# Attention slots, idle products and early copies in a fused attention and double-MLP kernel

## The chip, the cores and the metric

The kernel runs on one core of a Trainium2 chip. A core has a matrix engine (TensorE, PE in the profile; PEld is its weight load), a vector engine (VectorE, DVE), an activation engine (ScalarE, ACT), GpSimd (POOL) and a sync engine (SP). Each runs its own queue of instructions in order and waits on semaphores for the others. Transfers are issued from the SP, ACT and POOL queues and carried by 16 DMA engines. The metric is device time in microseconds (us); lower is better. A profile is one execution recorded by the hardware.

## The reference

The inputs are float64 arrays; the MLP weights reach the kernel in that form and it takes them apart itself. The work, cut to what matters:

```python
# q, k, v: 4 batches, 8 heads, 576 positions, 64 wide
scores = q @ k.T / 8, kept where 0 <= row - column < 64, else -1e9
x = softmax(scores) @ v                        # to 2304 tokens x 512
x = (silu(x @ w_gate) * (x @ w_val)) @ w_out   # first MLP, 512 -> 1536 -> 512
out = (sigmoid(x @ w_gate2) * (x @ w_val2)) @ w_out2   # second MLP
```

## The kernel before

The 2304 tokens are 18 attention blocks of 128. The first MLP works on five tiles of 4, 3, 4, 4 and 3 blocks (`BLOCKS`, line 69): 512, 384, 512, 512 and 384 tokens, called tile 0 to tile 4 here. Every operand of a product is split into a high and a low part, and a product is three products of parts (high by high, low by high, high by low), each over four chunks: 12 matrix instructions for one gate, value or output step.

The first four blocks are computed ahead of tile 0, in the order that the string `START` writes out (two letters for a step, a number for the block; `wm` is a number of products on a tile of zeros that nobody reads, lines 899 to 901). From then on time is counted in *slots*. A tile has 36 of them, three for each of twelve feature chunks: gate product (slot number divisible by 3), value product, output product (of the chunk before). Slots run through tile 0 (0 to 35), tile 1 (36 to 71), tile 2 (72 to 107) and so on. Extra work is hung on a slot by `at(...)`: `before` is issued ahead of the slot's product, `during` right behind it, `after` behind the activation that follows. Within a list, entries with `first=True` come first. Since each engine runs its queue in order, a slot number fixes what stands ahead of what, not when it runs.

While one tile runs, the blocks of the next are prepared in its slots (`plan_attention`, line 500). With a block's base slot `base`: scores in `base+2` (`scores`, L246), masks on DVE (L265), exponentials on ACT (L283), division by the sums (`normalize`, L304 on ACT for blocks 4 to 7, L308 on DVE for others), transposes of the two weight halves on PE (`transpose_p`, L316) with a copy out on ACT (`evacuate_p`, L322), the product with the values (`pv`, L332), and the split of its result into x: the high half on ACT (`x_hi`, L342), then the low half on DVE (`x_lo`, L345), which needs the high one. Only after `x_lo` is the bank of `pv` free. Transposes, `pv` and scores share two PSUM banks named `att` in turn, so the fourth piece of a sequence such as transpose, transpose, pv, scores, scores waits until the pieces before it have been read.

For blocks 8 to 17, q and k are first copied in DRAM into a layout of 32 by 32 squares (`to_squares`, line 131; 16 copies for each of batches 1, 2 and 3, each of two DMAs of 128-byte runs) and turned by DVE (`turn`, L233). These copies, the raw weights (`load_raw`, L373, four buffers), the reloads of the first MLP's output words (`reload`, L421) and the stores of prepared words all go through SP's queue. The raw words of the second MLP's output matrix are fetched one by one in tile 1 (loop at line 657: load, conversion by ACT L391, L394 and DVE L404 to L406, store).

The second MLP follows tile 4 and is not touched.

Of the kernel before, what the change touches and what calls it, by code (L numbers as in the profile page):

```python
# [28 lines left out]
tk0 tq0 tq1 ek0 eq0 se0 so0 me0 mo0 tk1 xe0 eq1 tk2 ek1 ne0 so1 xo0 tq2 se1 ek2 mo1 ca0 no0 eq2  # L29
so2 xo1 pe0 po0 me1 we0 mo2 cb0 xo2 xe1 se2 me2 no1 wo0 wm2 ca1 no2 ne1 tq3 vp0 po1 tk3 pe1 ek3  # L30
ch0 ca2 cb1 eq3 wo1 vp1 so3 xe2 se3 mo3 me3 we1 ne2 xe3 pv0 hi0 po2 cl0 ch1 pv1 vp2 pe2 lo0 wm2
ne3 xo3 cb2 vp3 hi1 we2 lo1 no3 pe3 wm1 wo2 ca3 cb3 we3 ca4 pv2 hi2 po3 wo3 lo2 cb4 pv3 ch3 ca5
hi3 lo3 cb5 ch2 ch4 ch5 cl1 cl2 cl3 cl4 cl5
"""
SPLIT_EARLY = START.count("ca")
# [3 lines left out]
def attention_moe_moe(  # L39
# [301 lines left out]
    def x_hi(i, xt, col):  # L341
        nc.scalar.activation(out=xt[:, 0, :, col:col + 128], in_=st[i, "x"], func=ACTF.Copy)  # L342

    def x_lo(i, xt, col):
        nc.vector.tensor_tensor(  # L345
            out=xt[:, 1, :, col:col + 128],
            in0=st.pop((i, "x")),
            in1=xt[:, 0, :, col:col + 128].bitcast(FP32),
            op=ALU.subtract,
        )  # L350
# [88 lines left out]
    def x_tile():  # L439
        return x_p.tile([128, 2, CC, 512], FP32R, tag="x", name="x")  # L440
# [44 lines left out]
    before, during, after = {}, {}, {}  # L485
    xts = {}

    def x_of(t):
        if t not in xts:
            xts[t] = x_tile()  # L490
        return xts[t]

    def at(where, g, fn, *a, first=False):
        where.setdefault(g, []).append((not first, fn, a))
# [3 lines left out]
            fn(*a)  # L498

    def plan_attention(i, base, t, col):  # L500
        pv_at = 10 if t == 1 or (t > 2 and col == 0) else 9
        if base >= 2:
            at(during, base - (5 if i < TURN else 6), load_qk, i)
        at(during, base + 1 if i < TURN else base - 2, load_v, i)
        at(during, base + 5 if i <= TURN else base + 2, load_before, i)
        for nm in "qk":
            if i < TURN:
                at(before, base + 1, transpose_in, i, nm)
                at(before, base + 1, evacuate, i, nm)
            else:  # L510
                at(during, base - 1, turn, i, nm, first=nm == "k")
        at(before, base + 2, scores, i)
        at(after, base + 2, masked, i, 0, first=True)
        at(after, base + 3, masked, i, 1, first=True)
        at(after, base + 3, exps, i, 0, first=True)
        at(after, base + 3, exps, i, 1, first=True)
        at(after, base + (4 if i < TURN else 5), normalize, i, 0, first=i >= TURN)
        at(after, base + 5, normalize, i, 1, first=True)
        for par in range(2):
            at(before, base + 7 + par, transpose_p, i, par)  # L520
            at(before, base + 7 + par, evacuate_p, i, par)
        at(before, base + pv_at, pv, i)
        at(before, base + pv_at, lambda: x_hi(i, x_of(t), col))
        at(before, base + pv_at + 1, lambda: x_lo(i, x_of(t), col))


    for b in range(B):
        s = max(0, 128 * TURN - W - b * S)
        if s >= S:
            continue  # L530
        parts = [(nm, b, s, hp, par) for hp in range(HP) for par in range(2) for nm in "kq"]
        first = {1: 12, 2: 24, 3: 46}[b]
        for j, part in enumerate(parts):
            at(during, first + j, to_squares, *part)
    blk = BLOCKS[0]
    for t in range(NTL - 1):
        nb = BLOCKS[t + 1]
        for b in range(nb):
            plan_attention(blk + b, SPT * t + {4: 9 * b - 3, 3: 12 * b - (3 if t else 0), 2: 18 * b + 3}[nb], t + 1, b * 128)
        blk += nb  # L540
# [115 lines left out]

    for fc, g in enumerate((39, 41, 43, 46, 48, 50, 52, 57, 59, 61, 66, 68)):
        key = (1, "o", fc)
        at(during, g - 5, load_raw, key)
        at(during, g - 1, round_a, key)  # L660
        at(during, g, round_b, key)
        at(during, g + 1, store, key)
# [229 lines left out]
    with tc.manual_schedule():  # L892
# [4 lines left out]
        t = ps_m.tile([128, 512], FP32, tag="a3", name="warm")  # L897
# [8 lines left out]
        for step in LOADS.split():  # L906
            nm, j = step[0], int(step[1:])
# [43 lines left out]
        g = 0  # L951
# [87 lines left out]
```

## Time and profile before

| | us |
|---|---|
| median of 3 runs | 967.22 (966.86 to 968.52) |
| profiled execution, its own time | 967.57 |
| its span | 965.8 |
| PE busy | 944.8 (98%) |
| DVE busy | 616.1 (64%) |
| ACT busy | 464.2 (48%) |

The span is what the profiler sees between the first and the last instruction; the profiled execution took 1.8 us more than that. A busy PE is counted with modelled ends, so a product that waits for its predecessor still counts as busy. The chain of waits is followed back from the last instruction; a wait of PE is time that nothing else can give back, as long as no other engine sets the pace there.

### The profile page before, as it was taken

The page shows a single profiled execution, that of the slowest core. Times are in us where ns is not written, and L with a number is a line of the kernel's source. Part 1 is how long each engine was busy: PE and PEld are TensorE (multiplying, and loading weights), DVE is VectorE, ACT ScalarE, POOL GpSimd, SP SyncE. Part 2 cuts the span into 40 slices and gives each one's busy share as a digit, 9 for nine tenths or more (in the row PEclk, how much of TensorE's full clock was granted, in tenths as well). Part 3 has the DMA queues.
Part 4 walks back from the last instruction along what each step waited for, and adds up shares of the span by engine and source line. Part 5 has one row for each costly group of instructions (what it writes and reads, how often), then busy time and mean ns, then how long its engine had stood idle before and what let it go on. Part 6 is the DMA issues. An engine that isn't in the chain of part 4 may idle for free.

```text
span 965.8 us, 15744 instructions
## 1 busy us (share of the span) xinstructions
PE 944.8 (98%) x5693; PEld 843.4 (87%) x5693; DVE 616.1 (64%) x1401; ACT 464.2 (48%) x1042; POOL 21.1 (2%) x39
## 2 busy tenths in 40 slices
PE   8799999999999999999999999999999999999998
PEld 6678887899878887888899999998999988999986
DVE  6889984565756556555565566687366685566842
ACT  6798995755644556445444322145211343222332
POOL 2102010000000000000000000000000000000000
PEclk7899999999999999999999999999999999999999
DMA  9778897999786665865599557725787536866411
GB/s 223 208 230 251 265 242 213 307 231 280 246 256 187 206 207 170 288 217 159 196 351 362 200 203 275 259 58 162 259 287 232 189 92 205 300 223 243 142 33 65
DMA packets 191773, 210.62 MB, mean 218 GB/s; under 512 B 93136, under 2 KB 135632, under 8 KB 191696
## 3 DMA queue, kind: packets, MB, share of 16 engines
q1 hardware_dynamic: 185360, 199.27, 65.9%
q10 hardware_dynamic: 5376, 7.21, 2.1%
q0 software_dynamic: 960, 3.15, 1.1%
q8 instruction: 45, 0.74, 0.3%
q14 instruction: 32, 0.26, 0.1%
HBM read 168.69 MB, written 46.40 MB: 223 GB/s over the span
## 4 chain that ended last, share of the span: by engine, by line
PE 87%; ACT 8%; DVE 2%; DMA 2%; issue 1%; ACTq 0%; DVEq 0%
PE a L781 14%; PE g L448 13%; PE a L459 13%; PE v L448 12%; PE att L781 7%; PE a L846 7%; PE att L846 3%; PE v L781 3%; PE g L781 3%; PE g L846 3%; PE v L846 3%; ACT z L283 2%; PE att L332 2%; PE att L246 1%; DMA raw<-in_moe_w_out_dram 1%; ACT L283 1%
## 5 line engine op out<-in xcount | busy, mean ns | idle before, releaser
L448 PE MATMUL g<-x,wg 128*128 128x512 f32 (+1 forms) x720 | 161.0, 372 | 0.9 <-ACT x L342 0.8
L459 PE MATMUL a<-h,wo 128*128 128x512 f32 (+1 forms) x720 | 161.3, 372 | 0.0
L448 PE MATMUL v<-x,wv 128*128 128x512 f32 (+1 forms) x720 | 160.2, 371 | 0.0
L448 PEld LDWEIGHTS g<-x,wg 128*128 128x128 f32 x720 | 131.6, 189 | 19.8 <-ACT s L961 1.0
L459 PEld LDWEIGHTS a<-h,wo 128*128 128x128 f32 x720 | 129.5, 188 | 18.6 <-issue 1.9
L448 PEld LDWEIGHTS v<-x,wv 128*128 128x128 f32 x720 | 130.0, 188 | 16.3
L781 PE MATMUL a<-xs,wop 128*128 128x384 f32 x756 | 136.2, 334 | 0.0
L781 PEld LDWEIGHTS a<-xs,wop 128*128 128x128 f32 x756 | 131.5, 188 | 0.1
L968 DVE TENSOR_TENSOR s<-s,v 128x512 f32<-128x512 f32 (+1 forms) x60 | 38.0, 634 | 119.0 <-PE v L448 90.8
L773 ACT ACTIVATE s<-s 128x384 f32<-128x384 f32 x72 | 37.9, 526 | 81.9 <-DVE s L767 81.7
L781 PE MATMUL att<-xs,wop 128*128 128x384 f32 x384 | 71.7, 334 | 0.0
L846 PE MATMUL a<-wo,hs 128*128 128x512 f32 x288 | 71.2, 389 | 0.0
L961 ACT ACTIVATE s<-g 128x512 f32<-128x512 f32 (+1 forms) x60 | 33.3, 554 | 78.8 <-PE g L448 78.3
L970 ACT ACTIVATE h<-s 128x512 fp32r<-128x512 f32 (+1 forms) x60 | 35.1, 586 | 71.0 <-DVE s L968 70.8
L781 PEld LDWEIGHTS att<-xs,wop 128*128 128x128 f32 x384 | 67.1, 188 | 0.1
L846 PEld LDWEIGHTS a<-wo,hs 128*128 128x128 f32 x288 | 54.0, 188 | 11.1
L404 DVE TENSOR_SCALAR raw<-raw 128x512 uint16<-128x512 uint16 x72 | 54.6, 759 | 4.3 <-ACT raw L391 4.0
L283 ACT ACTIVATE z<-z,nm 128x128 f32<-128x128 f32 x144 | 55.8, 390 | 2.3 <-DVE nm L265 2.1
L391 ACT ACTIVATE raw<-raw 128x512 int32<-128x512 uint32 x72 | 48.4, 672 | 7.3 <-DMA raw<-in_moe_w_out_dram 5.5
L406 DVE CUSTOM_DVE_ANT_0 t<-raw,t 128x1024 uint16<-128x1024 uint16 x72 | 49.9, 694 | 2.5
L767 DVE TENSOR_TENSOR s<-s,a 128x384 f32<-128x384 f32 x65 | 35.1, 553 | 22.9 <-PE a L781 22.6
L430 ACT ACTIVATE wo<-tw 128x512 fp32r<-128x512 f32 x36 | 22.6, 627 | 54.1 <-PE a L846 26.0
(130 smaller groups left out, 1290.6 us busy)
## 6 DMA issues: line engine op xcount, KB each, us to landing
wop<-wd SPq DMA_DIRECT2D x126, 512.0 KB, 6.0
wo<-k0o SPq DMA_DIRECT2D x48, 512.0 KB, 4.9
wd<-stage SPq DMA_DIRECT2D x36, 512.0 KB, 5.1
raw<-in_moe_w_gate_dram SPq DMA_DIRECT2D x24, 512.0 KB, 5.5
raw<-in_moe_w_val_dram SPq DMA_DIRECT2D x24, 512.0 KB, 5.6
raw<-in_moe_w_out_dram SPq DMA_DIRECT2D x24, 512.0 KB, 5.1
tw<-k1o SPq DMA_DIRECT2D x36, 256.0 KB, 3.5
k0o<-wo ACTq DMA_DIRECT2D x12, 512.0 KB, 4.6
```

The source lines that it names most:

```text
L283: nc.scalar.activation(out=z[:, hp, :], in_=z[:, hp, :], func=ACTF.Exp, scale=-1.0, bias=nm[:, hp:hp + 1], accum_out=su[:, hp:hp + 1],)
L391: nc.scalar.activation(out=lower, in_=lower.bitcast(UINT32), func=ACTF.Copy, scale=2.0 ** -29)
L404: nc.vector.tensor_scalar(second, fourth, 0x8000, None, ALU.bitwise_and)
L406: nc.vector.tensor_tensor(out=t, in0=t, in1=lower, op=ALU.add)
L448: nc.tensor.matmul(out=ps[:, 0:n], lhsT=w[:, a, c, :], rhs=xt[:, b, c, 0:n], start=(j == 0), stop=(j == len(mm) - 1),)
L459: nc.tensor.matmul(out=acc[e][:, 0:n], lhsT=w[:, a, e * 128:(e + 1) * 128], rhs=h[:, b, 0:n], start=(fc == 0 and j == 0), stop=(fc == FC - ...
L767: nc.vector.tensor_tensor(out=to[out], in0=to[a], in1=ps, op=ALU.add)
L773: nc.scalar.activation(out=to[which], in_=to[which], func=ACTF.Sigmoid)
L781: nc.tensor.matmul(out=ps, lhsT=w[:, val, a, c, :], rhs=xops[op, b][:, c], start=(n == 0), stop=(n == len(mm) - 1),)
L846: nc.tensor.matmul(out=acc[e], lhsT=h[e // 3][:, a, e % 3 * 128:(e % 3 + 1) * 128], rhs=w[:, b], start=(fc == 0 and n == 0), stop=(fc == F ...
L968: nc.vector.tensor_tensor(out=s, in0=s, in1=vps[:, 0:n], op=ALU.mult)
L970: nc.scalar.activation(out=h[:, 0, 0:n], in_=s, func=ACTF.Copy)
```

## The change

Six things are edited. (1) `START`: six idle products ahead of block 3's `pv`, three behind it. (2) Transposes of the weights: in tile 1's slots (blocks 7 to 10) both halves in `base+8` instead of `base+7` and `base+8`, and `pv` in `base+10` instead of `base+9`; for the first block of tiles 3 and 4 (blocks 11 and 15) one slot later each. (3) `pv` of block 6, the last block prepared in tile 0, in slot 33 instead of 34. (4) `x_lo` of blocks 6 to 17 first in `during` of the slot of `pv`, instead of `before` the next slot. (5) The copies in squares: batch 1 in slots 10 to 24 (was 12 to 27), batch 2 in 25 to 41 (24 to 39), batch 3 in 46 to 77 (46 to 61). (6) The loads of the second MLP's output words two slots earlier; their conversions stay.

```diff
 START:
-... ca4 pv2 hi2 po3 wo3 lo2 cb4 pv3 ch3 ca5
+... ca4 pv2 hi2 po3 wm6 wo3 lo2 cb4 pv3 wm3 ch3 ca5

     def plan_attention(i, base, t, col):
-        pv_at = 10 if t == 1 or (t > 2 and col == 0) else 9
+        if t == 1:
+            turn_at, pv_at = (7, 8), 9 if col == 256 else 10
+        elif t == 2:
+            turn_at, pv_at = (8, 8), 10
+        elif col == 0:
+            turn_at, pv_at = (8, 9), 10
+        else:
+            turn_at, pv_at = (7, 8), 9
...
         for par in range(2):
-            at(before, base + 7 + par, transpose_p, i, par)
-            at(before, base + 7 + par, evacuate_p, i, par)
+            at(before, base + turn_at[par], transpose_p, i, par)
+            at(before, base + turn_at[par], evacuate_p, i, par)
         at(before, base + pv_at, pv, i)
         at(before, base + pv_at, lambda: x_hi(i, x_of(t), col))
-        at(before, base + pv_at + 1, lambda: x_lo(i, x_of(t), col))
+        if t == 1 and col < 256:
+            at(before, base + pv_at + 1, lambda: x_lo(i, x_of(t), col))
+        else:
+            at(during, base + pv_at, lambda: x_lo(i, x_of(t), col), first=True)
...
-        first = {1: 12, 2: 24, 3: 46}[b]
+        first, last = {1: (10, 24), 2: (25, 41), 3: (46, 77)}[b]
         for j, part in enumerate(parts):
-            at(during, first + j, to_squares, *part)
+            at(during, first + j * (last - first) // (len(parts) - 1), to_squares, *part)
...
-        at(during, g - 5, load_raw, key)
+        at(during, g - 7, load_raw, key)
```

(`t` counts the tile whose blocks are prepared: `t == 1` is done in tile 0's slots, `t == 2` in tile 1's. Lines of the changed kernel from 500 on are numbered 7 to 10 higher.)

Three places in the queues. First ACT around slots 32 to 34, before: `pt1_1802` is the second weight half of block 6, `x_995` the x of tile 1, `s` the silu of slot 33's gate product, `k0o10` a store that ACT issues.

```order
L322 ACTIVATE pt1_1802<-att_1797 128x512
L391 ACTIVATE raw_1653<-raw_1653 128x512
L394 ACTIVATE t_1819<-raw_1653 128x512
L417 DMA k0o10_1838<-wo_1792 128x1024
L961 ACTIVATE s_1843<-g_1822 128x512
L342 ACTIVATE x_995<-att_1845 128x4x128
L213 ACTIVATE qt_1868<-att_1863 128x512
L219 ACTIVATE kt_1875<-att_1870 128x4x128
```

And ACT at the same place in the changed kernel:

```order
L322 ACTIVATE pt1_1809<-att_1804 128x512
L391 ACTIVATE raw_1660<-raw_1660 128x512
L394 ACTIVATE t_1826<-raw_1660 128x512
L342 ACTIVATE x_1004<-att_1831 128x4x128
L417 DMA k0o10_1866<-wo_1799 128x1024
L971 ACTIVATE s_1871<-g_1849 128x512
L213 ACTIVATE qt_1878<-att_1873 128x512
L219 ACTIVATE kt_1885<-att_1880 128x4x128
```

The high half of block 6's x now stands ahead of the silu of slot 33's gate product and ahead of a store; the copy of its second weight half stands where it stood, with one slot less until `pv`.

Next ACT in tile 1, slots 48 to 52, before: `pt0` and `pt1` are the weight halves of block 8, `x` takes the high half of its result, the two `s` are the silu of slots 48 and 51.

```order
L961 ACTIVATE s_2350<-g_2331 128x384
L322 ACTIVATE pt0_2357<-att_2352 128x512
L391 ACTIVATE raw_2262<-raw_2262 128x512
L394 ACTIVATE t_2380<-raw_2262 128x512
L970 ACTIVATE h_2384<-s_2350 128x384
L322 ACTIVATE pt1_2391<-att_2386 128x512
L342 ACTIVATE x_2156<-att_2414 128x4x128
L391 ACTIVATE raw_2325<-raw_2325 128x512
L394 ACTIVATE t_2450<-raw_2325 128x512
L961 ACTIVATE s_2453<-g_2432 128x384
```

And in the changed kernel:

```order
L971 ACTIVATE s_2357<-g_2338 128x384
L391 ACTIVATE raw_2209<-raw_2209 128x512
L394 ACTIVATE t_2378<-raw_2209 128x512
L980 ACTIVATE h_2382<-s_2357 128x384
L322 ACTIVATE pt0_2389<-att_2384 128x512
L322 ACTIVATE pt1_2396<-att_2391 128x512
L391 ACTIVATE raw_2273<-raw_2273 128x512
L394 ACTIVATE t_2437<-raw_2273 128x512
L971 ACTIVATE s_2440<-g_2421 128x384
L342 ACTIVATE x_2188<-att_2442 128x4x128
```

Both copies now stand behind the conversion of a raw weight and the split of `h`, and one more conversion and the silu of slot 51 stand between them and the high half of x.

Last DVE around slots 76 to 80, before: `kt` and `qt` are the turned k and q of block 12, `x_3273` is the x of tile 3, written for block 11, `s_3254` the product of slot 79's value step.

```order
L233 STREAM_TRANSPOSE kt_3229<-k_3066 128x768
L233 STREAM_TRANSPOSE qt_3231<-q_3064 128x512
L888 TENSOR_TENSOR h_3204<-s_3172,h_3204 128x512
L622 TENSOR_TENSOR stage_3249<-t_2985,stage_3249 128x256
L404 TENSOR_SCALAR raw_3132<-raw_3132 128x512
L405 TENSOR_SCALAR t_3251<-t_3251 128x512
L406 ISA t_3251<-raw_3132,t_3251 128x1024
L968 TENSOR_TENSOR s_3254<-s_3254,v_3275 128x512
L345 TENSOR_TENSOR x_3273<-att_3256,x_3273 128x4x128
```

And in the changed kernel:

```order
L233 STREAM_TRANSPOSE kt_3229<-k_3071 128x768
L233 STREAM_TRANSPOSE qt_3233<-q_3069 128x512
L898 TENSOR_TENSOR h_3204<-s_3179,h_3204 128x512
L345 TENSOR_TENSOR x_3282<-att_3265,x_3282 128x4x128
L632 TENSOR_TENSOR stage_3258<-t_2968,stage_3258 128x256
L404 TENSOR_SCALAR raw_3139<-raw_3139 128x512
L405 TENSOR_SCALAR t_3260<-t_3260 128x512
L406 ISA t_3260<-raw_3139,t_3260 128x1024
L978 TENSOR_TENSOR s_3263<-s_3263,v_3284 128x512
```

The low half of x has moved from behind the value step's multiplication to ahead of the staging and conversion work; the multiplication now stands behind it. Everything from the `stage` row on waits in this queue until `pv` of block 11 and its high half are done.

## Rows read from the trace of the kernel before

**Rows 1.** Windows by tile (engines' busy us, clock, DMA share, GB/s): tiles 0, 1, 2-4.

```profile
41.00:157.60 116.60, 114.66 (x700) 91.84 (x701) 98.70 (x232) 99.02 (x213) 15.07 (x15) 0.99 0.82 236
157.60:255.60 98.00, 94.15 (x734) 88.33 (x734) 58.70 (x163) 60.54 (x147) 0.00 (x0) 1.00 0.97 275
255.60:481.00 225.40, 223.27 (x1359) 182.48 (x1358) 128.85 (x319) 118.85 (x271) 0.00 (x0) 1.00 0.65 208
```

**Rows 2.** PE's waits from 41 us on: us in total, times, longest.

```profile
PE att L332 <- ACT pt L322: 3.4, 3, 1.6
PE att L246 <- DVE x L345: 2.3, 2, 1.2
PE att L316 <- DVE z L308: 1.4, 4, 1.0
...
PE att L204 <- ACT qt L213: 0.7, 1, 0.7
```

**Rows 3.** Timeline of PE, 36 to 46 us: start, us, instructions, [idle before].

```profile
38.92 1.15 PE L332 MATMUL a<-pt,v 128*64 128x64 f32 x32 [1.90 <-DVE x L345]
40.84 4.48 PE L448 MATMUL g<-x,wg 128*128 128x512 f32 x12 [0.76 <-ACT x L342]
45.15 0.60 PE L204 MATMUL att<-ident,q 128*128 128x128 f32 x4
```

**Rows 4.** Windows of the first gate product, then slots 0 to 8.

```profile
41.00:44.00 3.00, 3.00 (x8) 2.32 (x9) 2.97 (x6) 1.45 (x3) 0.00 (x0) 0.50 0.57 180
...
47.26:67.98 20.72, 20.66 (x120) 16.17 (x118) 17.00 (x46) 20.66 (x50) 2.79 (x3) 1.00 0.77 234
```

**Rows 5.** Chain of waits: start, us, what; unhindered groups of PE from their starts.

```profile
67.37 0.61 ACT s L961
...
68.03 3.02 PE g L448 x12
...
122.20 1.03 PE att L246 x32
...
146.54 1.08 PE att L332 x32
```

**Rows 6.** Timeline of PE, slots 33 to 35.

```profile
143.66 2.88 PE L448 MATMUL g<-x,wg 128*128 128x512 f32 x12
146.47 1.15 PE L332 MATMUL att<-pt,v 128*64 128x64 f32 x32
147.55 0.66 PE L204 MATMUL att<-ident,q 128*128 128x128 f32 x4
...
152.25 0.44 PE L246 MATMUL att<-kt,qt 64*64 64x128 f32 x4
...
154.79 3.02 PE L459 MATMUL a<-h,wo 128*128 128x512 f32 x12
```

**Rows 7.** Timeline of ACT, 120 to 150 us.

```profile
127.91 0.68 ACT L391 ACTIVATE raw<-raw 128x512 int32<-128x512 uint32 x1 [0.69 <-DMA raw<-in_moe_w_gate_dram]
144.17 0.60 ACT L322 ACTIVATE pt<-att 128x512 f32<-128x512 f32 x1
```

**Rows 8.** Timeline of PE, slots 41 to 43.

```profile
172.20 0.33 PE L332 MATMUL att<-pt,v 128*64 128x64 f32 x2
...
175.21 2.35 PE L448 MATMUL g<-x,wg 128*128 128x384 f32 x12
177.40 2.24 PE L448 MATMUL v<-x,wv 128*128 128x384 f32 x12
```

**Rows 9.** ACT's waits for raw weights, 41 to 260 us: total, times, longest.

```profile
ACT raw L391 <- DMA raw<-in_moe_w_out_dram: 5.5, 5, 1.8
```

**Rows 10.** Timelines of ACT and DVE around slot 79.

```profile
274.71 0.59 ACT L342 ACTIVATE x<-att 128x512 fp32r<-128x512 f32 x1
...
276.55 0.69 DVE L968 TENSOR_TENSOR s<-s,v 128x512 f32<-128x512 f32 x1 [0.99 <-PE v L448]
277.16 0.68 DVE L345 TENSOR_TENSOR x<-att,x 128x512 fp32r<-128x512 f32 x1
```

More of the change, by code (lines that the diff above doesn't have):

```diff
@@ L31 @@
 ch0 ca2 cb1 eq3 wo1 vp1 so3 xe2 se3 mo3 me3 we1 ne2 xe3 pv0 hi0 po2 cl0 ch1 pv1 vp2 pe2 lo0 wm2
-ne3 xo3 cb2 vp3 hi1 we2 lo1 no3 pe3 wm1 wo2 ca3 cb3 we3 ca4 pv2 hi2 po3 wo3 lo2 cb4 pv3 ch3 ca5
+ne3 xo3 cb2 vp3 hi1 we2 lo1 no3 pe3 wm1 wo2 ca3 cb3 we3 ca4 pv2 hi2 po3 wm6 wo3 lo2 cb4 pv3 wm3 ch3 ca5
 hi3 lo3 cb5 ch2 ch4 ch5 cl1 cl2 cl3 cl4 cl5
```

## The prediction

> **What bounds the kernel now.** I read three views in this order: busy time by stage, PE's waits, and the timeline around each wait. By stage, PE is busy for 114.66 of 116.60 us in tile 0, 94.15 of 98.00 in tile 1 and 223.27 of 225.40 in tiles 2 to 4 [rows 1]. Nothing else is near that but ACT, 99.02 of 116.60 in tile 0. So PE sets the time, and what it can still win is its waits. From 41 us on these are short and few [rows 2]: three times on a copied-out weight half ahead of `pv` (3.4 us), twice on `x_lo` ahead of scores (2.3), four times on normalized weights ahead of transposes (1.4), once ahead of block 7's transposes (0.7). That is 7.8 us of idle, all of it before the second MLP, which stays as it is. The edits aim at exactly these ten waits, and at one slow stretch of the clock: after a wait of 1.90 us and one of 0.76 us [rows 3] the granted clock stands at 0.50, the 1.2 GHz level, for the first gate product [rows 4].
>
> An idle time understates its wait. The `pv` of slot 42 takes 175.21 - 172.20 = 3.01 us from its first matmul to the next product [rows 8]; an unhindered one takes 1.08 [rows 5]. That is 1.93 lost, against the 1.6 that the wait list shows as its longest: 0.3 more. Scores of slot 35 take 154.79 - 152.25 = 2.54 [rows 6] against 1.03 [rows 5]: 1.51 lost, 0.3 more than the longest 1.2 in the list. I add 0.3 for each wait of these two kinds and nothing for the others, where I have no such pair.
>
> **The change part by part.**
>
> *Idle products at the start.* Six stand in the 1.90 us wait, three in the 0.76 us wait [rows 3]. An estimate from the unhindered gate product, 12 matmuls of the same shape in 146.47 - 143.66 = 2.81 us [rows 6], is 0.23 each: 1.4 and 0.7 us, so both groups fit their waits. If they hold the clock up, the first gate product takes 2.81 instead of 45.15 - 40.84 = 4.31 us [rows 3]: 1.5 us won there. I count none of it. From 47.26 to 67.98 ACT is busy for 20.66 of 20.72 us [rows 4], and the gate product at 68.03 starts right behind the silu that ends that stretch [rows 5]; ACT's start there is given by DVE's splits, not by PE. PE would come 1.5 us sooner and wait for it. Bounds: 1.5 won if something in that stretch gives way, 1.5 lost if the new wait lets the clock fall once more for as long as it did.
>
> *Block 6 in slot 33, its `x_lo` in the same slot.* The transposes of block 7 no longer share a slot with `pv` (0.7 won [rows 2]), and the scores of slot 35 no longer stand behind an `x_lo` that comes after the value step (1.51). But `pv` now needs the second weight half a slot sooner. ACT starts that copy at 144.17 and takes 0.60 us [rows 7]; PE is at the start of slot 33 at 143.66 [rows 6]: a new wait of 1.1 us. ACT waited 0.69 us for a raw gate weight at 127.91 [rows 7], which in the queue stood behind copies of two batches at once; these no longer overlap. If that wait goes, the new one is 0.4. I take 0.7, between them, and win 0.7 + 1.5 - 0.7 = 1.5 (1.1 to 1.8). Behind the `pv` that waits stands all of PE's queue, so it counts in full.
>
> *Tile 1, `pv` one slot later, both transposes together.* The wait of slot 42 goes (1.93), and two more of its kind: 3.4 - 1.6 = 1.8 us of idle plus 2 x 0.3, so 2.4. One slot is a product of at least 177.40 - 175.21 = 2.19 us [rows 8], longer than any of the three waits, so none is left over. In slot 42 it is near: ACT's second copy comes behind one conversion more than before, and I leave that at nothing. The three transposes in tile 1 and the one of block 15 get a slot more too: 1.4 us [rows 2], with no restart counted. What is late next is `x_lo`: it stands in DVE's queue where it stood, but its `pv` is one slot later, and the scores follow in the next slot. Behind `pv`, ACT's high half (0.59) and DVE's subtraction (0.68) take 1.3 us [rows 10], the product beside them 2.19. So this costs nothing unless ACT is held up by 0.9 us; the bound is 4 x 0.4 us if it is.
>
> *`x_lo` first in its slot, tiles 2 and 4.* At slot 79 the high half of x starts at 274.71, but `x_lo` runs at 277.16, behind the value step's multiplication at 276.55 [rows 10]. First in its slot it would start at 275.3 and end at 276.0, ahead of the end of the value product that the multiplication at 276.55 waited for, and with it of the scores behind that product. That wait goes: 2.3 - 1.1 of the one in slot 35, 1.2, plus 0.3: 1.5. In the other blocks nothing waits for it. What it holds up: staging, conversions and the multiplication, about 1.5 us later than now, which the low split two slots on covers.
>
> *Copies and loads.* No instruction is added. ACT waits five times for output words, 5.5 us in all, at most 1.8 [rows 9]; two slots are 4.4 us in tile 1. These waits are beside PE's products and count only through the copies ahead of `pv`, which have their slot already. Nothing for them; 1 us won or lost as bounds.
>
> The rule that speaks against the copies' new places: the Trainium skill (DMA: Bandwidth & Descriptors, Specifications) puts 512 bytes as the smallest transfer at full rate, and these runs are 128 bytes. By that they cost the same in any slot, and tile 1 is lighter by only three parts of 20; no run here shows a run of another length.
>
> The sum: 0 + 1.5 + 1.93 + 2.4 + 1.4 + 1.5 = 8.7 us. The profiled execution took 967.57 us (span 965.8 and 1.8 around it): 958.9. It stands 0.35 above the median of the three runs, so 958.5. I predict 958.6.
>
> **The rivals.**
>
> *Tile 1 is held by the DMA engines.* Its DMA share is 0.97 at 275 GB/s [rows 1], the highest of all tiles. Were that the limit, PE's waits there (1.93 + 2.4 + 0.5 of the transposes) would come back as later reloads and q and k: 4.8 less, 963.4. Against it: none of PE's waits names a transfer [rows 2].
>
> *The start is kept.* If ACT's stretch shortens too, 1.5 us more: 957.1. Against it: ACT is busy in it without a break.
>
> *The slow clock comes back* at the new wait before the first scores: 1.5 lost: 960.1. Tile 1 had waits of 1.6 us at a mean clock of 1.00 [rows 1, 2], which speaks against it. The Trainium skill (TensorE: Matmul & The Clock Gate, HAM oscillation) says that idling between groups of matmuls throttles PE again; the start's 1.90 us agree with it, the 1.6 us in tile 1 do not.
>
> *`x_lo` blocks DVE (slower).* In twelve blocks DVE stops at `x_lo` until `pv` and the high half are done, with conversions and the multiplication behind it. If the 1.5 us by which these come later reach PE every time, through the low split of `h` that the output product needs: 12 x 1.5 = 18 lost, 976.8. It decides once the split is late by more than the two slots (4.4 us) that it has; DVE, busy for 58.70 of 98.00 and 128.85 of 225.40 us [rows 1], would have to fall behind by three times as much as I expect.
>
> *The moves do nothing*, because the releasers named are only the last of several, and another is as late: 967.
>
> **How the numbers follow.** Forecast 0.66, with its own range 957.2 to 960.5; DMA 0.13; start kept 0.08; slow clock 0.05; DVE blocked 0.03; nothing 0.05. The range runs from the start kept with all restarts (956.0) to the near side of the DMA case (962.8). A measurement of this kernel tells 0.2%, 1.9 us, from no change: faster 0.92, same 0.05, slower 0.03.
>
> **What would show it.** Right: no wait of PE on L322 or on `x_lo` L345 after 157 us, one new wait of 0.3 to 1.1 us ahead of `pv` in slot 33, clock 1.00 during the first gate product and yet the gate product of slot 9 at about 68 us; tile 1 near 93 us. Wrong: waits on `x_lo` in slots 44, 53, 62 or 71, PE waiting for `h` or a reload, a clock below 1.00 behind 47 us, or tile 1 still at 96 us or more with a DMA share near 1.

## The result and the profile after

The changed kernel takes 958.54 us, median of 6 runs (957.52 to 961.99), against 967.28 for the kernel before, run beside it (966.39 to 970.48): ratio 0.9914, 95% interval 0.9890 to 0.9937. The forecast was 958.6 with a range of 956.0 to 962.8. The total was right; the term for copies and loads was not, since part of what they win stood in the sum under the name of another edit. The profiled execution took 957.52 us, 10.05 less than the one of before; 0.52 of that is an earlier first product and not counted to the change, since it scatters by more between executions (see the last section).

The page of the kernel after, its span and busy times:

```profile
span 955.7 us, 15746 instructions
...
PE 940.6 (98%) x5702; PEld 841.4 (88%) x5702; DVE 614.4 (64%) x1401; ACT 464.0 (49%) x1042; POOL 20.9 (2%) x39
```

Windows of the kernel after, cut at the same slots as those of [rows 1] (same columns; the third one ends, there as here, a few slots into tile 4):

```profile
40.48:155.80 115.32, 112.94 (x701) 90.75 (x701) 98.43 (x232) 98.99 (x213) 14.96 (x15) 1.00 0.83 243
155.80:248.20 92.40, 92.40 (x734) 87.96 (x733) 57.39 (x163) 60.15 (x147) 0.00 (x0) 1.00 0.96 272
248.20:470.90 222.70, 222.70 (x1359) 182.33 (x1358) 128.64 (x319) 118.98 (x271) 0.00 (x0) 1.00 0.69 217
```

They are 1.3, 5.6 and 2.7 us shorter than before; tile 1 takes 92.4 us, where the prediction said "near 93". PE has no idle time left in the last two windows; before it had 3.85 and 2.13 us there [rows 1]. All of PE's waits from 41 us to 950 us, kernel after (total, times, longest):

```profile
PE att L246 <- ACT kt L219: 1.5, 1, 1.5
PE att L332 <- ACT pt L322: 0.7, 1, 0.7
```

The ten waits of [rows 2] are gone; these two are new. The timeline of PE after shows them in their places, and three places where a wait has been:

```profile
40.31 2.98 PE L448 MATMUL g<-x,wg 128*128 128x512 f32 x12
43.13 0.60 PE L204 MATMUL att<-ident,q 128*128 128x128 f32 x4
...
48.42 1.10 PE L246 MATMUL att<-kt,qt 64*64 64x128 f32 x32 [1.52 <-ACT kt L219]
...
67.47 1.90 PE L448 MATMUL g<-x,wg 128*128 128x512 f32 x7
...
143.18 0.33 PE L332 MATMUL att<-pt,v 128*64 128x64 f32 x2
144.24 1.15 PE L332 MATMUL att<-pt,v 128*64 128x64 f32 x30 [0.73 <-ACT pt L322]
145.31 0.96 PE L448 MATMUL g<-x,wg 128*128 128x512 f32 x3
...
151.87 1.10 PE L246 MATMUL att<-kt,qt 64*64 64x128 f32 x32
...
172.40 1.15 PE L332 MATMUL att<-pt,v 128*64 128x64 f32 x32
...
269.02 1.10 PE L246 MATMUL att<-kt,qt 64*64 64x128 f32 x32
```

The first gate product is 43.13 - 40.31 = 2.82 us, where it was 4.31 [rows 3]. The gate product of slot 9 starts at 67.47 against 68.03 [rows 5], which is the earlier start alone: the 1.5 us are given back, but at slot 2, in a wait for `kt`, ACT's copy of the turned k. Scores of slot 35 (151.87) and `pv` in tile 1 (172.40) run without the gaps of [rows 6] and [rows 8].

To place the gain, I compared the start of every product of the two profiled executions, slot by slot. Gains by stretch, without the 0.52 of the start, beside the prediction's terms:

| stretch | measured us | predicted us |
|---|---|---|
| slots 0 to 2, idle products | 1.50 - 1.46 = 0.0 | 0 |
| slots 33 to 35, block 6 | 1.30 | 1.5 |
| slots 36 to 43, first `pv` of tile 1 | 2.03 | 1.93 |
| slots 44 to 70, two `pv` and the transposes of tile 1 | 0.37 + 1.66 + 1.52 = 3.55 | 2.4 + 0.4 |
| slots 71 to 80, `x_lo` | 1.49 | 1.5 |
| slots 81 to 115, block 15 | 1.08 | 1.0 |
| copies and loads | in the rows above | 0 |

### The profile page after: what moved, and what is told of

It is laid out like the page before. It is cut to its first block, busy times and chain, and to the rows that moved or that the text cites. A ratio compares the mean times of both kernels' runs of the same rounds, so it can differ in the third digit from the quotient of the medians.

```text
span 955.7 us, 15746 instructions
## 1 busy us (share of the span) xinstructions
PE 940.6 (98%) x5702; PEld 841.4 (88%) x5702; DVE 614.4 (64%) x1401; ACT 464.0 (49%) x1042; POOL 20.9 (2%) x39
## 4 chain that ended last, share of the span: by engine, by line
PE 91%; ACT 6%; DVE 2%; DMA 0%; issue 0%; ACTq 0%; SPq 0%; DVEq 0%
PE g L448 14%; PE a L459 14%; PE a L791 14%; PE v L448 14%; PE att L791 7%; PE a L856 7%; PE att L856 3%; PE v L791 3%; PE g L791 3%; PE g L856 3%; PE v L856 3%; PE att L332 2%; PE att L246 1%; ACT z L283 1%; PE att L316 1%; ACT raw L391 1%
```

## The experiments

Times are medians; each ratio is to the kernel before, run beside the kernel on the same chip (966.3 to 967.1 us). The start-up ends up to 3.7 us earlier or later from one execution to the next, so profiled executions are compared **from the first product on**: span minus the start of the first gate product. That is 924.96 us before and 915.39 after, 9.57 less. Each kernel has one such trace.

**1. The idle products, taken out of the changed kernel.**

```
-... po3 wm6 wo3 lo2 cb4 pv3 wm3 ch3 ca5
+... po3 wo3 lo2 cb4 pv3 ch3 ca5
```

> The changed kernel without its nine idle products. Theory: the clock falls to 1.2 GHz for the first gate product (4.3 us instead of 2.82 from its start to the next transposes), but PE then waits about 1.5 us less for kt in slot 2, and the gate product of slot 9 starts about 27.2 us after that of slot 0, as in both kernels; the time stays within 0.5 us of the changed kernel's 958.5. Rival, the clock's gain is kept: 1.5 us more, 960.0, with slot 9 1.5 us later against slot 0.

Measured: 959.71 us, ratio 0.9925 (0.9904 to 0.9946). The median stands nearer to the rival's 960.0, but the interval does not tell it from the changed kernel's 0.9914; the trace decides. From the first product on it is 955.3 - 39.35 = 915.95, 0.56 more. PE's timeline:

```profile
39.35 4.41 PE L448 MATMUL g<-x,wg 128*128 128x512 f32 x12 [0.76 <-ACT x L342]
43.60 0.60 PE L204 MATMUL att<-ident,q 128*128 128x128 f32 x4
...
47.49 1.10 PE L246 MATMUL att<-kt,qt 64*64 64x128 f32 x32
```

The gate product is 1.43 us longer again, at a mean granted clock of 0.64 (1.00 in the changed kernel), and the wait at slot 2 is gone: 1.40 us come back there. In the changed kernel the idle products hold the clock up and keep nothing.

**2. What took it back: the store of the o word's parts, put off to slot 1.** In the changed kernel ACT waits 2.15 us for DVE before its first silu, and `kt` stands behind it. The kernel before has the same wait. Timeline of ACT, kernel before and then after:

```profile
45.96 1.28 ACT L961 ACT_TABLE_LOAD   x1 [2.16 <-DVE wo L434]
```

```profile
45.41 1.28 ACT L971 ACT_TABLE_LOAD   x1 [2.15 <-DVE wo L434]
...
47.67 0.60 ACT L219 ACTIVATE kt<-att 128x512 f32<-128x512 f32 x1
```

```
-  split_lo(convs[j][1]) or (convs[j][1][1] == "o" and store_parts(convs[j][1])),
+  split_lo(convs[j][1]) or (convs[j][1][1] == "o" and at(during, 1, store_parts, convs[j][1])),
```

> The changed kernel with one thing more: the store of the last converted output word's parts, for which ScalarE waits 2.2 us on VectorE at the end of the start-up, is put off to slot 1. What the idle products won at the start (1.50 us) was given back 1.46 us in a wait of TensorE for ScalarE's copy of kt at slot 2. Theory: ScalarE's queue at the start holds that gain back, so with 2.2 us less in it the wait of 1.5 us at 48.4 us goes and the kernel is at 957.0 to 957.5 us. Rival: what ScalarE does until 68 us is work and not that wait, so the gain is again given back at a later slot (by slot 9) and the time stays at 958.5.

Measured: 955.84 us, ratio 0.9890 (0.9864 to 0.9915). From the first product on 956.0 - 42.04 = 913.96, 1.43 less than the changed kernel. PE and then ACT of this kernel:

```profile
42.04 3.02 PE L448 MATMUL g<-x,wg 128*128 128x512 f32 x12
...
48.59 1.10 PE L246 MATMUL att<-kt,qt 64*64 64x128 f32 x32
```

```profile
44.39 0.63 ACT L430 ACTIVATE wg<-t 128x512 fp32r<-128x512 f32 x1 [1.37 <-DVE t L406]
45.04 1.28 ACT L971 ACT_TABLE_LOAD   x1
```

The table load follows without the wait, the scores of slot 2 wait for nothing, and by slot 3 the kernel is 1.55 us nearer to its first product than the changed one; nothing of it is lost again by slot 9. So the prediction's reason, that ACT is busy without a break until 68 us, was not what bound it: the break stood ahead of the stretch that I read.

**3. The same without the idle products.** The two edits of 1 and 2 together.

> The kernel with the late store of the o word's parts (955.8 us) without the idle products. With the early store the idle products kept nothing of the 1.4 us that they won, since ScalarE gave it back in the wait for kt. Theory: with 2.2 us less in ScalarE's queue the gain is kept, so taking the products out here costs 1.4 us: first product of the first MLP about 4.3 us, no wait for kt at slot 2, and 957.0 to 957.5 us. Rival: there is no more to be had at the start than the late store gave, and the time is 955.8 again.

Measured: 959.13 us, ratio 0.9918 (0.9897 to 0.9938); from the first product on 956.6 - 40.05 = 916.55, 2.59 more than experiment 2. Of that, 1.49 are lost at slot 1 and not given back at slot 3: with ACT free, the idle products are worth their 1.5 us. The other 1.16 are one wait at slot 80 that experiment 2 had not. It follows a store of staged weights to DRAM (`wd<-stage`), out of a buffer that ACT writes next: it took 6.44 us from issue to landing, 5.57 in experiment 2. ACT and PE there, this kernel:

```profile
266.63 0.42 ACT L627 ACTIVATE stage<-t 128x256 fp32r<-128x256 f32 x1 [3.94 <-DMA wd<-stage]
...
268.53 0.59 ACT L342 ACTIVATE x<-att 128x512 fp32r<-128x512 f32 x1
```

```profile
269.90 1.09 PE L246 MATMUL att<-kt,qt 64*64 64x128 f32 x28 [0.74 <-DVE x L345]
```

In the changed kernel ACT waits 2.52 us at this place, x's high half starts at 267.42, and `x_lo` ends at 268.72, 0.3 us ahead of the scores at 269.02. So the `x_lo` of slot 80 has some 0.3 us to spare, and a store that lands later uses it up. Experiments 10 and 11 lose 0.9 and 1.0 us at the same place; whether by scatter or by their edits, one trace each does not show.

**4. `x_lo` back in its old place, in the changed kernel.**

```
-        if t == 1 and col < 256:
+        if True:
             at(before, base + pv_at + 1, lambda: x_lo(i, x_of(t), col))
```

> The changed kernel with x_lo ahead of the slot behind pv, as before, all else as changed. Theory: x_lo runs behind the value step's multiplication where pv is in a value slot, so the scores that follow wait: the 1.6 us of slot 80 come back, and four new waits of the same size open in slots 44, 53, 62 and 71, since pv there now stands one slot ahead of the scores: 8 us more, 966.5. Rival, only the places that waited before matter: 1.6 us more, 960.1.

Measured: 965.09 us, ratio 0.9975 (0.9962 to 0.9989), 6.6 more than the changed kernel. From the first product on 964.9 - 41.90 = 923.00, 7.6 more: 1.46 to 1.47 at each of slots 44, 53, 62 and 71, and 1.60 at slot 80. PE's waits:

```profile
PE att L246 <- DVE x L345: 5.3, 5, 1.2
```

The theory holds, with 7.6 of its 8 us by the trace: the later `pv` needs the earlier `x_lo`.

**5. `x_lo` first, alone, in the kernel before.**

```
-        at(before, base + pv_at + 1, lambda: x_lo(i, x_of(t), col))
+        if t == 1 and col < 256:
+            at(before, base + pv_at + 1, lambda: x_lo(i, x_of(t), col))
+        else:
+            at(during, base + pv_at, lambda: x_lo(i, x_of(t), col), first=True)
```

> The kernel before with one part of the change alone: x's lower half right after its upper half, first on VectorE in the slot of the product with the values (for the blocks that the change moves). Of the change's terms this alone should take the waits of the scores at slots 35 and 80 (1.5 and 1.6 us from start to start) and leave the others: theory 3.1 us less from slot 81 on, 963.5 to 964.5 us against 966.3 to 967.1 for before. Rival: VectorE, first in its queue waiting for the values' product, holds the normalization behind it, new waits of TensorE for z appear, and the time is that of before or longer.

Measured: 966.89 us, ratio 1.0006 (0.9993 to 1.0019): no change, and neither theory. The trace has both gains, 1.51 at slot 35 and 1.60 at slot 80, and no new wait worth naming for z; another 1.15 are won at slot 69, whose wait is missing here. But 0.87 us are lost by slot 31 and 1.72 + 1.04 at slots 60 and 61; in all 0.3 are left. ACT's waits for output words there, then its queue, then PE's:

```profile
ACT raw L391 <- DMA raw<-in_moe_w_out_dram: 6.6, 3, 3.3
```

```profile
218.38 0.65 ACT L391 ACTIVATE raw<-raw 128x512 int32<-128x512 uint32 x1 [3.04 <-DMA raw<-in_moe_w_out_dram]
```

```profile
220.54 1.60 PE L332 MATMUL att<-pt,v 128*64 128x64 f32 x30 [2.19 <-ACT pt L322]
222.07 3.42 PE L448 MATMUL g<-x,wg 128*128 128x384 f32 x12
```

PE is 1.16 us ahead of the kernel before at slot 49 (0.77 of it an earlier first product), the word is not (it landed at 218.35, before at 218.20), ACT stops at the word 1.2 us longer than before (3.04 against 1.8 [rows 9]), and the weight's copy for `pv` stands behind it. So what PE was ahead became a wait for a transfer. That the edit did it, and not scatter of the start and of the word, is not shown by one trace; the median of 11 runs only says that nothing of the gain is left.

**6. Turns in their old slots, in the changed kernel** (transposes and `pv` of tile 1, blocks 11 and 15; `x_lo`, copies and loads stay new).

```
-            turn_at, pv_at = (8, 8), 10
+            turn_at, pv_at = (7, 8), 9
         elif col == 0:
-            turn_at, pv_at = (8, 9), 10
+            turn_at, pv_at = (7, 8), 10
```

> The changed kernel with transposes and pv of tiles 1, 2 (first block) and 3 (first block) in their old slots; x_lo stays first in the slot of pv, loads stay early. Theory that the slot removes each wait: 2.0 us in slot 42, 1.3 and 1.2 in slots 60 and 69, 0.37 in slots 49, 58 and 67, 1.1 in slot 112 come back: 6.7 more, 965.2. Rival, the early loads alone remove the waits of slots 60 and 69, because ACT stood at a late word just ahead of these copies: 4.2 more, 962.7.

Measured: 962.06 us, ratio 0.9951 (0.9936 to 0.9966). From the first product on 957.9 - 38.24 = 919.66, 4.27 more than the changed kernel: 2.12 at slots 41 to 43, 0.35 to 0.37 per block at slots 49 to 70, 1.12 at block 15. PE's waits:

```profile
PE att L332 <- ACT pt L322: 2.3, 2, 1.6
...
PE att L316 <- DVE z L308: 0.5, 3, 0.2
```

One wait of 1.6 for `pt` is back, that of slot 42. The waits of slots 60 and 69 stay away though `pv` stands in its old slot there. The rival holds: they are no matter of the slot.

**7. The loads two slots earlier, alone, in the kernel before.**

```
-        at(during, g - 5, load_raw, key)
+        at(during, g - 7, load_raw, key)
```

> The kernel before with one part of the change alone: the loads of the second MLP's output words two slots earlier. Theory: the waits of TensorE at slots 60 and 69 in tile 1 (1.3 and 1.15 us) are the words' lateness passed on through ScalarE and not the slot of the last block's values, so loads alone remove them: 964.5 to 965 us, ScalarE's waits for these words (5.5 us in 5) gone. Rival: the slot decides, the waits stay, and the time is that of before, 967.0.

Measured: 964.79 us, ratio 0.9979 (0.9963 to 0.9995). The trace is 1.25 us shorter at slot 60 and 1.15 at slot 69, 0.3 longer at each of slots 7 and 58, and has nothing else of the change; ACT has no wait for an output word. PE's waits:

```profile
PE att L332 <- ACT pt L322: 1.6, 1, 1.6
```

Beside [rows 2]: of three waits for `pt` one is left. So 2.4 us of the trace belong to the loads (1.5 by medians). How a late word holds up the copies for `pv` is seen in experiment 8.

**8. Copies and loads, both back in the changed kernel.**

```
-        first, last = {1: (10, 24), 2: (25, 41), 3: (46, 77)}[b]
+        first = {1: 12, 2: 24, 3: 46}[b]
...
-            at(during, first + j * (last - first) // (len(parts) - 1), to_squares, *part)
+            at(during, first + j, to_squares, *part)
...
-        at(during, g - 7, load_raw, key)
+        at(during, g - 5, load_raw, key)
```

> The changed kernel with the copies in squares and the loads of the second MLP's output words in their old slots. Theory that the slots of transposes and pv took the waits of tile 1 away: ACT waits for raw words again (about 5 us in all) but no wait of PE comes back, 958.5 to 959.5. Rival, late words set the waits: the two waits of 0.9 us in slots 60 and 69 come back, 961; or the DMA engines hold tile 1, up to 4.8 us more, 963.3.

Measured: 965.16 us, ratio 0.9983 (0.9970 to 0.9996): 6.6 more than the changed kernel, more than any of the expected. From the first product on 964.0 - 40.08 = 923.92, 8.5 more: 0.65 at slot 44, 1.68 at slot 50, 4.53 at slot 61, 1.51 at slot 62. ACT and then PE of this kernel ahead of slots 61 and 62, and the window of the product behind the wait:

```profile
213.54 0.49 ACT L971 ACTIVATE s<-g 128x384 f32<-128x384 f32 x1
219.96 0.66 ACT L391 ACTIVATE raw<-raw 128x512 int32<-128x512 uint32 x1 [5.93 <-DMA raw<-in_moe_w_out_dram]
220.52 0.66 ACT L394 ACTIVATE t<-raw 128x512 f32<-128x512 f32 x1
221.07 0.52 ACT L980 ACTIVATE h<-s 128x384 fp32r<-128x384 f32 x1
221.49 1.07 ACT L322 ACTIVATE pt<-att 128x512 f32<-128x512 f32 x2
```

```profile
222.13 2.45 PE L332 MATMUL att<-pt,v 128*64 128x64 f32 x32 [3.16 <-ACT pt L322]
224.51 3.87 PE L448 MATMUL v<-x,wv 128*128 128x384 f32 x12
```

```profile
224.51:228.31 3.80, 3.80 (x14) 3.54 (x13) 2.09 (x4) 1.65 (x4) 0.00 (x0) 0.56 0.93 261
```

Read in this order: a word lands after ACT has come to it, ACT stands still for 5.93 us, both copies of `pt` stand behind it, PE waits 3.16 us even though `pv` has its later slot, and the clock is low for the next two groups (`pv` 2.38 us to the next start instead of 1.08, the product 3.80 instead of 2.19).

**9. Only the copies back, and 10. only the loads back**, each one half of the diff of 8.

> The changed kernel with only the copies in squares (to_squares) back in their consecutive slots; the word loads stay two slots earlier. With copies and loads both back the kernel lost 6.6 us, and its trace had ScalarE waiting 15.9 us for words of the second MLP's output weight (5.9 the longest). Theory: the place of the loads decides, since such a load landed about 6 us after its issue and is wanted two slots of some 2.1 us sooner than that allows; then this kernel stays at 958.5 to 959.5 us and the word waits stay under 1 us each. Rival: the copies, which stand in the same issue queue and take the DMA engines, decide; then it is at 963 to 965 us with word waits of 4 to 6 us around 210 to 225 us.

> The changed kernel with only the loads of the second MLP's output words back at five slots ahead of the slot they are for; the copies in squares stay spread. Theory (the loads' place decides): 963 to 965 us, with ScalarE's waits for these words back, 10 us or more in total. Rival (the copies decide): 958.5 to 960 us, word waits at most those of before (5.5 us in 5). If both are needed at once, each of the two kernels alone loses only 1 to 3 us, and the 6.6 is not their sum.

Measured: copies back 962.73 us, ratio 0.9962 (0.9947 to 0.9977); loads back 959.22, ratio 0.9919 (0.9900 to 0.9938). From the first product on 959.1 - 38.21 = 920.89 and 957.9 - 40.00 = 917.90, that is 5.5 and 2.5 more than the changed kernel; of the 2.5, 0.88 are at slot 80. ACT's wait, PE and the clock with the copies back:

```profile
217.84 0.69 ACT L391 ACTIVATE raw<-raw 128x512 int32<-128x512 uint32 x1 [5.11 <-DMA raw<-in_moe_w_out_dram]
```

```profile
220.85 1.09 PE L246 MATMUL att<-kt,qt 64*64 64x128 f32 x28 [2.24 <-DVE x L345]
221.87 3.93 PE L459 MATMUL a<-h,wo 128*128 128x384 f32 x12
```

```profile
221.87:225.64 3.77, 3.77 (x14) 3.77 (x13) 3.19 (x19) 0.52 (x1) 0.00 (x0) 0.55 0.90 231
```

And ACT's waits with the loads back:

```profile
ACT raw L391 <- DMA raw<-in_moe_w_out_dram: 6.0, 2, 5.7
```

My theory, that the place of the loads decides, fell: the copies are the larger part (though with the loads back ACT still waits up to 5.7 us for a word, which the rival did not expect). Together the two cost more than their sum by medians, 6.6 against 4.2 + 0.7; by the trace it is 8.5 against 5.5 + 1.6, without slot 80. Why the copies weigh so much is seen in the transfers from 200 to 226 us: all packets, then the loads of output words, with the median us from issue to landing at the end. First the changed kernel, then the kernel of experiment 8:

```profile
DMA packets 11986, 7.21 MB, mean 277 GB/s; under 512 B 9512, under 2 KB 10536, under 8 KB 11985
...
raw<-in_moe_w_out_dram SPq DMA_DIRECT2D x3, 512.0 KB, 6.4
```

```profile
DMA packets 14832, 6.18 MB, mean 238 GB/s; under 512 B 12709, under 2 KB 13733, under 8 KB 14831
...
raw<-in_moe_w_out_dram SPq DMA_DIRECT2D x3, 512.0 KB, 4.9
```

In these 26 us the copies back in consecutive slots issue 19 loads into squares (`qs`, `ks`) where the spread ones issue 10. More packets of under 512 bytes go with fewer bytes moved, at a DMA share of 0.93 (0.98 in the changed kernel). But the words are not slower under way: 4.9 us against 6.4. They are issued later. The load of the word for slot 61, which stands in slot 54 in the changed kernel and in that of experiment 9, on SP's queue, changed kernel first:

```profile
207.20 0.56 SPq L373 DMA_DIRECT2D raw<-in_moe_w_out_dram  x1
```

```profile
212.27 0.56 SPq L373 DMA_DIRECT2D raw<-in_moe_w_out_dram  x1
```

From the first gate product that is 166.88 and 174.06 us: SP comes to this load 7.2 us later, in slot 59 and not in slot 56, and it lands 5.55 us after its issue (6.83 in the changed kernel). So the copies make the word late by standing ahead of it in SP's queue. What SP loses at each copy, its own issuing or the engines behind it, is not measured apart.

**11. Block 6's `pv` back in slot 34**, in the changed kernel.

```
-            turn_at, pv_at = (7, 8), 9 if col == 256 else 10
+            turn_at, pv_at = (7, 8), 10
```

> The changed kernel with the product with the values of block 6 back in slot 34 (its x_lo still first in its slot). The prediction counted 1.5 us for taking the old wait of slot 35 away and 0.7 for the new one in slot 33; the changed kernel's trace has that new wait at 0.73 us of idle and 1.05 from start to start. Theory: back in slot 34 it costs no wait, x_lo lands in time because it is first, and the profiled run is 0.7 to 1.0 us shorter from slot 35 on. Rival: the wait moves to the scores of slot 35 or to the next block's transposes and is as long, so the total of waits stays within 0.3 us. The median itself can't tell 0.7 us well; the trace decides.

Measured: 958.55 us, ratio 0.9914 (0.9898 to 0.9930). 0.22 us won over slots 33 and 34; further on 1.02 lost at slot 80, as in experiment 3. PE's wait there:

```profile
PE att L204 <- ACT qt L213: 0.7, 1, 0.7
```

The rival holds: block 7's transposes wait again, as long as `pv` did.

**12. The late store and `pv` in slot 34 together.** The edits of 2 and 11.

> Both edits together: the late store and block 6's product with the values in slot 34. If the two waits are separate (their places are 95 us apart) the gains add: TensorE has no wait over 0.3 us from 41 us on, and the kernel is at 955.0 to 955.5 us, 0.7 to 1.0 us under the late store alone. Rival: the wait of 0.7 us moves on within tile 1 and the time is that of the late store, 955.8.

Measured: 956.04 us, ratio 0.9886 (0.9868 to 0.9903); from the first product on 953.0 - 39.27 = 913.73, 0.23 less than the late store alone. The one wait of PE left:

```profile
145.76 0.66 PE L204 MATMUL att<-ident,k 128*128 128x128 f32 x4 [0.69 <-ACT qt L213]
```

No gain that can be measured over the late store alone, as the rival said. Experiments 2 and 12 are the shortest kernels of this study, 2.5 to 2.7 us under the changed one by medians and 1.4 to 1.7 by the trace; the intervals of their ratios overlap that of the changed kernel, so the trace is what shows it.

## Why the prediction was right, and where it was not

*What bounds.* Right: PE sets the time and its waits were what could be won. All ten went.

*Idle products, counted at nothing.* The size was right: 1.50 won, 1.46 given back. The step was wrong in its place. The prediction held ACT's unbroken work from 47.26 to 67.98 to be the bound and looked for the loss at slot 9. It came at slot 2, and ACT had a break of 2.15 us just ahead of that stretch, which the same sentence had noted ("ACT's start there is given by DVE's splits") without asking whether the wait had to stand there. With that wait moved the 1.5 us are kept (experiments 2 and 3), which is the prediction's bound of 1.5 won "if something in that stretch gives way".

*Block 6 and slot 33.* Predicted 1.5, measured 1.30. The new wait has 0.73 us of idle, 0.7 predicted, but from start to start it costs 145.31 - 143.18 - 1.08 = 1.05: the 0.3 that the prediction added to every old wait of this kind it did not add to the new one.

*`pv` in tile 1.* Slot 42: 1.93 predicted, 2.03 measured, and experiment 6 has it back at 2.12 when the slot is undone. Slots 60 and 69: the 2.4 were there, but the prediction gave them to the wrong edit. The loads alone remove them (experiment 7), and undoing the slot does not bring them back (experiment 6).

*Copies and loads, counted at nothing with 1 us as bounds.* This is the term that failed. The sentence was: "These waits are beside PE's products and count only through the copies ahead of `pv`, which have their slot already." In the changed kernel these edits hold 6.6 us of medians, 8.5 of the trace (experiment 8). The later slot of `pv` covers short waits of ACT for a word: three of 0.8 to 1.5 us cost PE nothing in experiment 8. With the copies unspread ACT stops at a word for 5 to 6 us, and then the slot does not cover it. SP comes to the load for slot 61 no sooner than in the kernel before (174.1 us from the first product with the copies back, 173.5 with both, 172.2 before), while PE at slot 59 is 3.8 and 1.6 us ahead. The bounds were drawn from ACT's waits before, at the pace that PE had before. What the spread copies alone would do in the kernel before was not run. What I worked out beside the Trainium skill (DMA: Bandwidth & Descriptors, Specifications: 512 bytes as the smallest transfer at full rate), that the copies cost the same in any slot, fell too. The rule itself agrees with the packet lines above, where more small packets go with 238 in place of 277 GB/s; what the slots changed is how many of them stand in front of a word that is wanted. The count that the prediction gave, tile 1 lighter by three parts of 20, is two (18), and a count by tile misses that batch 3 goes from one part in every slot to about one in two.

*The total was right all the same* because the sum was taken against the kernel before. There the late words cost 2.4, which the sum contained under another name; the larger loss arises only when PE is made faster without the copies and loads. That the median met the forecast to 0.1 us is luck: from the first product on the gain is 9.6, not 8.7, mostly by the transposes, and medians of six runs scatter by more than the difference.

*The rival that the DMA engines hold tile 1* (0.13, 963.4) described a real bound, though what the trace shows is the order of SP's queue and not slower loads. Without the copies' and loads' edits it would have decided: 965.16, and with the copies alone back 962.73. What I held against it, that no wait of PE named a transfer, was no evidence: PE waited for ACT, and ACT for the transfer [rows 9].

*Transposes.* 1.4 predicted, about 1.1 in tile 1 (three times 0.35 to 0.37, experiment 6) and 1.1 to 1.2 at block 15 measured: 0.8 more, since no restart was counted.

*`x_lo`.* 1.5 predicted at slot 80, 1.49 measured. That a later `pv` without an earlier `x_lo` would wait, bounded at 4 x 0.4 us, is 4 x 1.46 when `x_lo` is not first (experiment 4). With it first, the blocked DVE of the slower rival cost nothing: PE's wait list has no wait for `h`.

*The slow clock.* It did not return behind the new waits of 1.52 and 0.73 us; tile 0 stands at 1.00. That tile 1's waits of 1.6 us had left the clock alone was weak evidence all the same, since waits of one length did both at the start (last section).

*Small sums.* The terms give 958.5, and 958.6 was forecast; 18 us more than that are 976.6, not 976.8. Neither touches a term.

## What to carry to other kernels

When a change makes the bounding engine faster, the lateness of a transfer must be read again at the new pace: take each load's landing against the moment at which its user will now want it, through the engine that stands between. Then look whether a late one was slow under way or issued late, behind what stands ahead of it in its queue. A wait list that names no transfer for the bounding engine says nothing until the waits of the engine it names are read too. And where a gain is given back, look at the one break in the queue that gives it back, also just ahead of the stretch in which that queue seems full.

## What the hardware showed beside this

The start-up, up to the first gate product, ended between 38.21 us (experiment 9) and 41.90 us (experiment 4) in profiled executions of kernels that have the same start-up. The changed kernel's six runs spread over 4.5 us; that the start makes most of that is likely but not measured, since only one of the six was profiled. Medians of six runs can't settle 1 us here. A trace from the first product on can, if it is read slot by slot: its total still has scatter such as the 1 us at slot 80.

The clock: behind PE's waits of 1.52 us (slot 2, kernel after) and 1.59 us (experiment 6) the granted clock stays at 1.00, the 2.4 GHz level. Behind 1.90 and 0.76 us at the start before [rows 3, 4], 2.19 us (experiment 5), 2.24 us (experiment 9) and 3.16 us (experiment 8) it falls: the next products run at a mean of 0.50 to 0.64, near the 1.2 GHz level, and take 1.1 us longer (experiment 5), 1.6 (experiment 9) or, over two groups, 2.9 (experiment 8). From start to start the waits of 2.19 and 2.24 us cost 4.0 and 4.2, and the one of 1.59 cost 1.9, with no slower product behind it. The length alone does not decide: in the start-up the granted clock fell to 0.50 behind a wait of 2.01 us (before the `pv` at 30.98, kernel after) and stayed at 1.00 behind 2.21 us (31.20, experiment 10) and 2.17 us (31.19, experiment 11).
